# Projections of two chunks with keys, queries and values by turns

## The chip, the cores and the metric

The kernel runs on one core of a Trainium2 chip. The metric is the device time of one execution in microseconds (us); the median of the runs counts.

## The reference

The kernel computes one transformer block in float32 for 2048 tokens of width 640: attention with 32 heads of width 20, then a gated feed-forward part of width 1728. In the reference, cut to what matters here:

```python
x = A_x                                   # 1 x 2048 x 640
qkv = layernorm(x) @ wqkv                 # 640 x 1920: queries, keys, values
scores = einsum("bhqd,bhkd->bhqk", q, k) * 20 ** -0.5
o = softmax(scores) @ v
h = x + o @ wo
out = h + (silu(layernorm(h) @ w_gate) * (layernorm(h) @ w_up)) @ w_down
```

## The kernel before

**Three stages.** First the projections, up to 337 us of the profile's span: layernorm, transposes, and the product with `wqkv`. Then attention, unit by unit (a unit is a group of four heads and a chunk of 512 queries; there are 8 groups and 4 chunks). Then the output projection and the feed-forward part. The change is in the first stage alone.

**Chunks and slots.** The 2048 tokens are worked in four chunks of 512, numbered 0 to 3. The loop over a chunk (from L503) goes through a list `work` of 18 entries; an entry is called a slot here, and `slot[0] = 18 * c + j` counts them over all chunks. An entry is either a block or a value. A *block* (`query_key`, L414) computes 128 rows of keys or queries for the chunk: fifteen matmuls of 128x512 into one bank `ps_one`, as each factor is split into a high and a low part and three of the products are kept. Even blocks are keys, odd ones are queries; there are five of each. A *value* (`value`, L451) computes 128 tokens by 320 columns of values: fifteen matmuls of 128x320. There are eight of them in a chunk. Before, chunks 1 and 2 go through all keys (slots 0 to 4), all queries (5 to 9) and all values (10 to 17). Chunk 0 has queries and keys in pairs, and chunk 3 has keys, values, queries; neither is changed.

**What follows a block.** `keep` (L432) takes the next of three tiles `e` by turns (`next_e`; two own tiles and a part of `v_stk`). ACT copies the bank into it (L265), rounds it to the high part (L80), and POOL subtracts for the low part (L81). The rows go to the DRAM tensor `qk_d` in two or three DMAs on ACT's queue; `store` (L408) holds them back until the next slot's copies are issued. Values go to `v_d` in the same way through two tiles `ev` (L465), one store for two values.

**Norm and flips of the next chunk.** While chunk c is projected, DVE does the layernorm of chunk c + 1 in 15 small steps (`lns`): four of statistics, seven of the inverse root, four that apply it, one step a slot from slot 1 and two a slot from slot 5. Then, in slots 11 to 15 (`flip_at`), `flip` (L387) transposes a fifth of the normed chunk by four PE transposes into a bank `ps_one`; ACT copies it to a tile `e` (the same three by turns, L265), rounds it (L80) and POOL subtracts. There are two banks `ps_one` for blocks, values and flips together.

**Maxima by the way.** Softmax needs the maximum of the scores for each query. A part of them is worked here, to give DVE something to do: `max_pair` (L166) computes two heads' scores of 128 queries by 512 keys with two matmuls into a tile `ps_wide` (three of them by turns), and DVE reduces the tile (L175). This is called a pair. `visit(n)` (L342) tries n pairs: each slot has `visit(3)` at its end, and each block of chunks 1 to 3 has one more between its matmuls. The pairs come in a fixed order from two lists, `urgent` (the unit of group 0 and chunk 0) and `early`. For groups 1 to 7 keys and queries are read back from `qk_d` into four tiles `raw`, by `load_items` on SP's queue in four DMAs each (`stack`, L143). `stored_at` (L274) gives the slot from which a tile may be read back; a tile is loaded when the tile four places earlier in the list has had its last pair, and counts as ready two slots later. A visit whose first pair isn't ready does nothing. A pair of `early` thus waits in the program for its slot, and on the chip for its tile.

**Loads for attention.** `load_keys(0, ...)` at slot 3 and `load_queries(c)` at slot 8 read group 0's keys and queries of this chunk back from `qk_d`, on SP's queue as well.

The order of each engine's instructions is the program's order; there is no scheduler. The kernel's functions with the profile's line numbers:

Of the kernel before, what the change touches and what calls it, by code (L numbers as in the profile page):

```python
# [23 lines left out]
ND = D // P  # L24
NT = S // P
CH = 512
NC = S // CH
# [16 lines left out]
def tile_block(ctx: ExitStack, tc: tile.TileContext, x, wqkv, wo, wg, wu, wd, out):  # L44
# [102 lines left out]
    def load_keys(g, cs=slice(0, S)):  # L147

        k = keys[g] = k_stk[g % 2]
        stack(k[:, :, cs], 1, g, cs)  # L150

    def load_queries(u):

        g, c = divmod(u, NC)
        q = queries[u] = stk.tile([P, 2, CH], F32R, name="q_stk", tag="q_stk", bufs=4)
        stack(q, 0, g, slice(c * CH, (c + 1) * CH))

    def load_values(g, t0=0, t1=NT):
        values[g] = v_stk[g % 2]
        nc.sync.dma_start(  # L160
            values[g][:, t0:t1], v_d[:, g].rearrange("(t p) w -> p t w", p=P)[:, t0:t1]
        )
# [40 lines left out]
    def max_finish(u):  # L203

        m = ps_one()[: 2 * G * TPC, :P]
        nc.tensor.transpose(m, ends.pop(u).bitcast(F32).rearrange("p i n -> p (i n)"), ident)
        m2 = stk.tile([2 * G * TPC, P], F32R, name="m2", tag="m2", bufs=1)
        nc.scalar.activation(m2, m, AF.Copy)
        for b in range(2):
            for i in range(2):  # L210
                row = b * ROW + NPART + i
                first = (2 * i + b) * 2 * TPC
                nc.sync.dma_start(
                    queries[u][row : row + 1].bitcast(F32).rearrange(
                        "r j (t p) -> r (j t) p", t=TPC
                    ),
                    m2[first : first + 2 * TPC, :].bitcast(F32),
                )
# [33 lines left out]
    with tc.tile_pool(name="pa", bufs=2) as pa:  # L252
# [5 lines left out]
        def load_x(c):  # L258
            for t in range(c * TPC, (c + 1) * TPC):
                xs[t] = pa.tile([P, D], F32, name="xt", tag="xt", bufs=4)  # L260
                nc.sync.dma_start(xs[t], x[t * P : (t + 1) * P, :])
# [12 lines left out]
        def stored_at(which, g, c):  # L274

            block = ((g + 1) * GD - 1) // P
            if c == 0:
                return 2 * block + 4
            return 18 * c + 3 + block + (0 if which else ND)

        def raw_tile():
# [7 lines left out]
        def load_items():  # L289
            for n, (which, g, c, loaded, _) in enumerate(items):  # L290
                if loaded is not None:
                    continue
                if slot[0] < stored_at(which, g, c) or (n >= 4 and users[n - 4]):
                    return
                t = raw_tile().rearrange("p a b -> p (a b)")[:, : 2 * CH].rearrange(
                    "p (h n) -> p h n", h=2
                )
                stack(t, which, g, slice(c * CH, (c + 1) * CH))
                items[n][3:] = t, slot[0]
# [42 lines left out]
        def visit(n):  # L342
            load_items()
            for _ in range(n):
                for queue in (urgent, early):
                    if queue and queue[0][0]():
                        queue.pop(0)[1]()
                        break
# [3 lines left out]
        def load_w(i):  # L352

            m, n = 2 * i, min(2, 3 * ND - 2 * i)
            raw = raw_tile().bitcast(F32)
            for j in range(n):
                raws[m + j] = raw[:, :, j * P : (j + 1) * P]
            nc.sync.dma_start(
                raw[:, :, : n * P], wqkv[:, m * P : (m + n) * P].rearrange("(k p) n -> p k n", p=P)
            )  # L360

        def split_w(m):
            cs = slice(m * P, (m + 1) * P)
            engine = nc.gpsimd if m % 2 == 1 else nc.vector
            split(raws.pop(m), w_hi[:, :, cs], w_lo[:, :, cs], engine)

        def norm(c):

            mv = pa.tile([P, TPC, 2], F32, name="mv")
            r, steps = rstd_steps(pa, mv[:, :, 1], TPC, "a")  # L370

            def apply(t):
                nc.vector.tensor_scalar(
                    xs[c * TPC + t], xs[c * TPC + t], mv[:, t, 0:1], r[:, t : t + 1],
                    op0=ALU.subtract, op1=ALU.mult,
                )

            zs[c] = (
                pa.tile([P, ND, CH], F32R, name="z_hi"), pa.tile([P, ND, CH], F32R, name="z_lo")
            )  # L380
            return (
                [lambda t=t: stats(pa, xs[c * TPC + t], mv[:, t, :]) for t in range(TPC)]
                + [lambda f=f, g=g: (f(), g()) for f, g in zip(steps[::2], steps[1::2])]
                + [lambda t=t: apply(t) for t in range(TPC)]
            )

        def flip(c, k):  # L387
            ps = ps_one()
            for t in range(TPC):
                nc.tensor.transpose(  # L390
                    ps[:, t * P : (t + 1) * P], xs[c * TPC + t][:, k * P : (k + 1) * P], ident
                )
            z_hi, z_lo = (z[:, k, :] for z in zs[c])
            split_sbuf(ps, z_hi, z_lo, next_e()[:, 0].bitcast(F32))
# [102 lines left out]
        parts = [("value", *divmod(i, 2)) for i in range(2 * TPC)]  # L497
        first = [("block", 0, 1), ("none",)] + [("block", m) for m in range(2, 2 * ND)]
        some_keys = [("block", 2 * i) for i in range(ND)]
        some_queries = [("block", 2 * i + 1) for i in range(ND)]  # L500
        flip_at = (12, 11, 11)
        finish_at = 18 * NC
        for c in range(NC):  # L503
            lns = []
            work = (some_keys + some_queries if c else first) + parts
            if c == NC - 1:
                work = some_keys + parts + some_queries

                es[:] = [e for e in es if e is not third]
                es.insert(1, pa.tile([P, ND, CH], F32R, name="z_hi")[:, :2])  # L510
            for j, (kind, *which) in enumerate(work):
                slot[0] = 18 * c + j
                if c == 0 and j < 9:
                    for i in range(split_at[j], split_at[j + 1]):
                        split_w(i + 2)
                        if i % 2 == 1 and loaded < 8:
                            load_w(loaded)
                            loaded += 1
                if j == 0 and c + 1 < NC:
                    if c > 0:  # L520
                        load_x(c + 1)
                    lns = norm(c + 1)
                if which:
                    (query_key if kind == "block" else value)(c, *which)
                visit(3)
                if c == 0 and j == 6:
                    for ev in evs:
                        nc.gpsimd.memset(ev, 1.0)
                if j == (4 if c == 0 else 3):
                    load_keys(0, slice(c * CH, (c + 1) * CH))  # L530
                if j == (4 if c == 0 else 8) and c < 3:
                    load_queries(c)
                if 0 in ends:
                    finish_at = min(finish_at, slot[0] + 2)
                    if slot[0] == finish_at:
                        max_finish(0)
                if j == 14 and c == 3:
                    load_values(0)
                for _ in range(2 if j >= 5 else 1):
                    if j >= 1 and lns:  # L540
                        lns.pop(0)()
                if c + 1 < NC and 0 <= j - flip_at[c] < ND:
                    flip(c + 1, j - flip_at[c])
                if c == NC - 1 and j == 11:
                    nc.scalar.activation(
                        pa.tile([P, 1], F32, name="exp_table"), eps_t, AF.Exp
                    )
# [420 lines left out]
    for u in range(NU):  # L968
        g, c = divmod(u, NC)
        if g == NG - 1 and c >= 2:  # L970
            _, first, ln, flips, _ = ahead
# [626 lines left out]
```

## Time and profile before

| what | us |
|---|---|
| median of three runs (2109.99 to 2112.93) | 2111.07 |
| the profiled execution: its time | 2112.34 |
| its span, first to last instruction | 2110.6 |
| chunk 1, first block matmul to that of chunk 2 (89.81 to 174.96) | 85.15 |
| chunk 2 (174.96 to 263.54) | 88.58 |
| chunk 3 and up to attention (263.54 to 337.42) | 73.88 |

A profile's busy time counts an instruction from its start to its end; matmuls overlap, so PE shows as busy even where each takes longer than it need. A wait in brackets is the idle time of that engine before the instruction, with what ended it. The granted clock is the share of TensorE's full clock.

### The profile page before, as it was taken

How to read it: one execution, taken by the hardware profiler on the slowest of the kernel's cores; microseconds unless marked ns; L12 is line 12 of the kernel's file. 1: busy time of each engine (PE TensorE's matmuls, PEld its weight loads, DVE VectorE, ACT ScalarE, POOL GpSimd, SP SyncE). 2: the span in 40 equal slices, each digit the busy share in tenths (PEclk: the TensorE clock that was granted, in tenths of full speed). 3: DMA queues.
4: the chain of work that ended last, by engine and by line, in shares of the span. 5: the costliest groups of instructions: out<-in, count | busy, mean ns of one | idle time of the engine just before them, and what ended most of it. 6: DMA issues, size and time to landing. Idle time of an engine off the chain costs nothing.

```text
span 2110.6 us, 35576 instructions
## 1 busy us (share of the span) xinstructions
PE 2077.2 (98%) x12606; PEld 1205.3 (57%) x12606; DVE 1752.9 (83%) x2901; ACT 1295.9 (61%) x2571; POOL 704.8 (33%) x1009
## 2 busy tenths in 40 slices
PE   7999999999999999999999999999999999999998
PEld 5766675333333333333333333335578888888887
DVE  6999997999999999999999999996358766666676
ACT  3222216999999999999999999996743222212221
POOL 3222212343343433353420001001135434653555
PEclk9999999999999999999999999999999999999999
DMA  7565432343433524533432113132137755884542
GB/s 253 168 190 166 153 119 82 122 122 106 150 115 102 169 89 136 165 136 126 136 110 75 33 38 88 33 100 76 35 121 262 266 171 186 300 299 158 197 152 92
DMA packets 199673, 295.27 MB, mean 140 GB/s; under 512 B 46840, under 2 KB 81656, under 8 KB 198472
## 3 DMA queue, kind: packets, MB, share of 16 engines
q1 hardware_dynamic: 185912, 266.77, 39.1%
q10 hardware_dynamic: 13584, 26.23, 4.0%
q8 instruction: 101, 1.65, 0.4%
q14 instruction: 76, 0.62, 0.1%
HBM read 196.44 MB, written 95.68 MB: 138 GB/s over the span
## 4 chain that ended last, share of the span: by engine, by line
PE 89%; DVE 5%; DMA 3%; POOL 1%; issue 1%; ACT 1%; SPq 0%; ACTq 0%; POOLq 0%; DVEq 0%
PE acc L900 24%; PE ps_max L181 15%; PE ps_one L890 15%; PE ps_a L1063 15%; PE ps_b L1157 8%; PE ps_one L422 4%; DVE mx L175 3%; PE ps_one L459 2%; PE ps_wide L171 2%; PE ps_max L628 2%; PE ps_b L628 1%; DMA qk_d<-e 1%; DMA raw<-qk_d 1%; DVE mx L187 1%; DMA halves<-j_d 1%
## 5 line engine op out<-in xcount | busy, mean ns | idle before, releaser
L896 ACT ACTIVATE probs<-ps_one 128x512 f32<-128x512 f32 x2048 | 1045.4, 623 | 131.9 <-PE ps_one L890 126.9
L187 DVE TENSOR_REDUCE mx<-ps_max 128x1 f32<-128x512 f32 x1632 | 1021.0, 683 | 95.7 <-PE ps_max L181 51.9
L890 PE MATMUL ps_one<-q_stk,k_stk 62*128 62x512 f32 x2048 | 551.1, 421 | 0.7 <-ACT e L265 0.7
L900 PE MATMUL acc<-probs,v_stk 128*32 128x512 f32 x4096 | 545.2, 604 | 0.3
L181 PE MATMUL ps_max<-k_stk,q_stk 60*128 60x512 f32 x1632 | 540.5, 459 | 2.4 <-DVE mx L187 1.5
L181 PEld LDWEIGHTS ps_max<-k_stk,q_stk 60*128 60x128 f32 x1632 | 230.2, 184 | 427.6 <-DVE mx L187 411.2
L890 PEld LDWEIGHTS ps_one<-q_stk,k_stk 62*128 62x128 f32 x2048 | 299.7, 185 | 81.6 <-ACT probs L896 52.3
L175 DVE TENSOR_REDUCE mx<-ps_wide 128x2 f32<-128x1024 f32 x208 | 240.5, 1217 | 16.2 <-PE ps_wide L171 16.0
L1278 DVE TENSOR_TENSOR tmp<-ps_a,tmp 128x512 f32<-128x512 f32 x208 | 141.2, 689 | 120.2 <-PE ps_a L1063 94.5
L1157 PE MATMUL ps_b<-halves,yp 128*128 128x320 f32 x1032 | 179.3, 308 | 1.8 <-POOL yp L81 1.2
L1157 PEld LDWEIGHTS ps_b<-halves,yp 128*128 128x128 f32 x1032 | 165.1, 188 | 18.4 <-POOL yp L81 1.5
L900 PEld LDWEIGHTS acc<-probs,v_stk 128*32 128x32 f32 x4096 | 80.6, 108 | 160.2 <-issue 152.1
L198 POOL CAST both<-neg 128x16 fp32r<-128x16 f32 x32 | 6.6, 206 | 467.6 <-DVE neg L194 212.5
L1063 PE MATMUL ps_a<-t,units 128*128 128x512 f32 x624 | 162.5, 396 | 0.0
L1063 PE MATMUL ps_a<-z,units 128*128 128x512 f32 x516 | 133.8, 394 | 0.0
L1063 PEld LDWEIGHTS ps_a<-t,units 128*128 128x128 f32 x624 | 112.6, 188 | 18.6
L81 POOL TENSOR_TENSOR yp<-y,yp 128x256 fp32r<-128x256 f32 x96 | 60.3, 628 | 187.8 <-ACT yp L80 187.8
L1162 DVE TENSOR_TENSOR h<-ps_b,h 128x320 f32<-128x320 f32 x248 | 110.1, 481 | 6.8 <-PE ps_b L1157 5.4
L1063 PEld LDWEIGHTS ps_a<-z,units 128*128 128x128 f32 x516 | 93.1, 187 | 15.9
L1063 PE MATMUL ps_a<-z,lasts 128*128 128x512 f32 x324 | 92.5, 393 | 0.0
L80 ACT ACTIVATE yp<-tmp 128x512 fp32r<-128x512 f32 x40 | 25.3, 632 | 103.2 <-POOL tmp L1150 103.2
L265 ACT ACTIVATE e<-ps_one 128x512 f32<-128x512 f32 x31 | 18.5, 598 | 107.3 <-PE ps_one L422 72.4
(164 smaller groups left out, 2066.6 us busy)
## 6 DMA issues: line engine op xcount, KB each, us to landing
units<-w_d SPq DMA_DIRECT2D x186, 256.0 KB
w_d<-stage SPq DMA_DIRECT2D x106, 256.0 KB
halves<-j_d SPq DMA_DIRECT2D x70, 320.0 KB
j_d<-stage SPq DMA_DIRECT2D x42, 320.0 KB
raw<-qk_d SPq DMA_DIRECT2D x70, 160.0 KB
k_stk<-qk_d SPq DMA_DIRECT2D x64, 160.0 KB
q_stk<-qk_d SPq DMA_DIRECT2D x64, 160.0 KB
rb<-r_d SPq DMA_DIRECT2D x32, 256.0 KB
```

The costliest lines, as they stand in the source:

```text
L175: nc.vector.tensor_reduce(mx[:, :, pair, t, kc], ps, axis=AX.X, op=ALU.max)
L181: nc.tensor.matmul(ps, queries[u][rows, pair, t * P : (t + 1) * P], keys[u // NC][rows, pair, kc * CH : (kc + 1) * CH], start=True, stop=True,
L187: nc.vector.tensor_reduce(mxs[u][:, b, pair, t, kc : kc + 1], ps, axis=AX.X, op=ALU.max)
L422: nc.tensor.matmul(ps, w[:, k, m * P : (m + 1) * P], a[:, k, :], start=(n == 0 and k == 0), stop=(n == 2 and k == ND - 1),)
L628: nc.tensor.matmul(ps[:, :HALF], a[:, k, :], w[:, k, hs], start=(n == 0), stop=(n == 3 * ND - 1),)
L890: nc.tensor.matmul(ps, keys[u // NC][rows, p, kt * P : (kt + 1) * P], queries[u][rows, p, :], start=True, stop=True,)
L896: nc.scalar.activation(probs[p][:, b, :], ps, AF.Exp, scale=scale)
L900: nc.tensor.matmul(acc[32 * j : 32 * j + 32, :], values[u // NC][:, kt, j * VW : j * VW + 32], probs[j // 2][:, j % 2, :], start=(kt == 0) ...
L1063: nc.tensor.matmul(ps.rearrange("p (t n) -> p t n", t=TPC), w[k][:, i], z[k][:, :, j], start=(first and m == 0), stop=(last and m == len(n ...
L1157: nc.tensor.matmul(ps, a, b, start=(n == 0), stop=(n == len(pairs) - 1))
L1162: nc.vector.tensor_tensor(out=h, in0=ps, in1=h, op=ALU.add)
L1278: add = lambda out, ps, x: nc.vector.tensor_tensor(out=out, in0=ps, in1=x, op=ALU.add)
```

## The change

The list of chunks 1 and 2 becomes key block, query block, value, five times over, and then the last three values; the slots in which a tile counts as stored are moved along, and `load_queries` is called at slot 5 instead of 8. Keys are now in slots 0, 3, 6, 9, 12, queries in 1, 4, 7, 10, 13, values in 2, 5, 8, 11, 14, 15, 16, 17. The steps of norm, the flips and the visits stay at their slot numbers.

```diff
             block = ((g + 1) * GD - 1) // P
             if c == 0:
                 return 2 * block + 4
+            if c < NC - 1:
+                return 18 * c + 3 + 3 * block + (0 if which else 1)
             return 18 * c + 3 + block + (0 if which else ND)
...
             lns = []
-            work = (some_keys + some_queries if c else first) + parts
+            work = first + parts
+            if c:
+                work = [a for block in zip(some_keys, some_queries, parts) for a in block]
+                work += parts[ND:]
             if c == NC - 1:
                 work = some_keys + parts + some_queries
...
-                if j == (4 if c == 0 else 8) and c < 3:
+                if j == (4 if c == 0 else 5) and c < 3:
                     load_queries(c)
```

## The prediction

> **What bounds the kernel now.** The page first.
>
> ```profile
> PE 2077.2 (98%) x12606; PEld 1205.3 (57%) x12606; DVE 1752.9 (83%) x2901; ACT 1295.9 (61%) x2571; POOL 704.8 (33%) x1009
> ```
>
> PE is busy nearly throughout, so a stall of PE anywhere lengthens the run one for one. The change touches only chunks 1 and 2 of the projections. Their stages are found in the time line of PE by the first block matmul of each chunk (89.81, 174.96 and 263.54 us) and the first value matmul (145.28 and 233.46); the view by stretches, cut there, has us, then busy us of PE, PEld, DVE, ACT and POOL, the granted clock, the DMA share and GB/s.
>
> ```profile
> 89.81:145.28 55.47, 53.09 (x230) 33.37 (x229) 51.75 (x67) 11.62 (x19) 11.55 (x9) 1.00 0.64 196
> 145.28:174.96 29.68, 29.08 (x191) 23.55 (x189) 28.69 (x28) 10.33 (x20) 7.77 (x6) 1.00 0.39 125
> 174.96:233.46 58.50, 55.50 (x232) 34.41 (x230) 52.22 (x68) 12.10 (x20) 11.58 (x9) 0.97 0.61 186
> 233.46:263.54 30.08, 29.45 (x190) 23.73 (x188) 29.11 (x28) 9.85 (x19) 7.74 (x6) 1.00 0.49 154
> ```
>
> Chunk 1 takes 85.15 us and chunk 2 takes 88.58. PE and DVE are both nearly full, ACT and POOL are far from it: the two run a race, slot by slot. The time line of PE gives the price of a slot (start, us, engine and line, count, idle before in brackets).
>
> ```profile
> 89.81 1.43 PE L422 MATMUL ps_one<-z_hi,w_hi 128*128 128x512 f32 x5
> ...
> 94.09 0.97 PE L171 MATMUL ps_wide<-raw 60*128 60x512 f32 x6
> 94.99 1.43 PE L422 MATMUL ps_one<-z_hi,w_hi 128*128 128x512 f32 x5
> ...
> 100.14 1.43 PE L422 MATMUL ps_one<-z_hi,w_hi 128*128 128x512 f32 x5
> ...
> 105.88 1.45 PE L422 MATMUL ps_one<-z_hi,w_hi 128*128 128x512 f32 x5
> ...
> 111.49 0.47 PE L171 MATMUL ps_wide<-raw 60*128 60x512 f32 x1 [0.56 <-DMA raw<-qk_d]
> 113.12 0.47 PE L171 MATMUL ps_wide<-raw 60*128 60x512 f32 x1 [1.17 <-DMA raw<-qk_d]
> 113.52 1.43 PE L422 MATMUL ps_one<-z_hi,w_hi 128*128 128x512 f32 x5
> ...
> 157.03 0.97 PE L459 MATMUL ps_one<-w_hi,z_hi 128*128 128x320 f32 x5
> ...
> 159.40 0.97 PE L171 MATMUL ps_wide<-k_stk,q_stk 60*128 60x512 f32 x6
> 160.30 0.66 PE L390 MATMUL ps_one<-ident,xt 128*128 128x128 f32 x4
> 160.71 0.97 PE L459 MATMUL ps_one<-w_hi,z_hi 128*128 128x320 f32 x5
> ...
> 208.35 1.42 PE L422 MATMUL ps_one<-z_hi,w_hi 128*128 128x512 f32 x5
> ...
> 213.03 0.46 PE L171 MATMUL ps_wide<-raw 60*128 60x512 f32 x1 [1.91 <-DMA raw<-qk_d]
> ...
> 213.76 2.04 PE L422 MATMUL ps_one<-z_hi,w_lo 128*128 128x512 f32 x5
> 215.73 1.65 PE L171 MATMUL ps_wide<-raw 60*128 60x512 f32 x6
> 217.31 1.50 PE L422 MATMUL ps_one<-z_hi,w_hi 128*128 128x512 f32 x5
> ```
>
> An undisturbed block slot with four max pairs takes PE 94.99 - 89.81 = 5.18 us, 5.17 below; its last three pairs take 0.90 (94.09 to 94.99). A value slot takes 2.37 + 0.90 = 3.28, a flip 0.41 more (160.30 to 160.71). A block slot after a stats step of the next chunk's norm takes 105.88 - 100.14 = 5.74: DVE sets it. Two slots are out of line: 105.88 to 113.52 is 7.64, and 208.35 to 217.31 is 8.96; both wait for a raw tile. The chain of waits tells why (start, us, what), with the table of the waits of SP's queue.
>
> ```profile
> 105.54 5.25 DMA qk_d<-e
> 110.80 2.08 DMA raw<-qk_d
> ...
> 144.37 3.40 DVE mx L175 x3
> ...
> 190.30 3.51 DMA qk_d<-e
> 193.87 3.83 DMA raw<-qk_d
> ...
> 202.53 4.19 DMA qk_d<-e
> 206.78 0.27 SPq L143
> ...
> 207.87 5.07 DMA raw<-qk_d
> ```
> ```profile
> SPq L143 <- DMA qk_d<-e: 32.0, 14, 4.3
> ```
>
> In the built program every DMA of SP and ACT takes one of eight completion semaphores by turns and first waits for the transfer eight places earlier. So a load of a raw tile on SP stands behind a store of keys on ACT which it doesn't need, and the store is issued only when the next block's matmuls have ended. It lands 3.5 to 5.25 us after its issue, the load 2.1 to 5.1 us after that.
>
> **The change, part by part.** Nothing is added or taken away: the order listing of both kernels gives the same matmuls, copies and DMAs in all. What moves: seven of the ten blocks and three values fall into slots 1 to 10 instead of nine blocks and one value, and the flips of slots 11 to 15 stand among a value, two blocks and two values instead of five values.
>
> *The race of PE and DVE.* A pair costs DVE 3.40 / 3 = 1.133 us, so a block's four 4.53 and a value's three 3.40. Chunk 1's 63 pairs are 71.4 of its 80.4 us of DVE, chunk 2's 64 are 72.5 of 81.3: norm costs 8.9, all of it in slots 1 to 10. There DVE needs, before, 9 x 4.53 + 3.40 + 8.9 = 53.1 against PE's 9 x 5.17 + 3.28 = 49.8; after, 7 x 4.53 + 3 x 3.40 + 8.9 = 50.8 against 46.0. DVE sets both. In slots 11 to 17 PE needs, before, 7 x 3.28 + 5 x 0.41 = 25.0 against DVE's 23.8; after, 2 x 5.17 + 5 x 3.28 + 5 x 0.41 = 28.8 against 26.1. PE sets both. With slot 0 (5.17) a chunk comes to 83.3 before and 84.8 after: 1.5 us dearer, as norm is now crowded beside shorter slots and PE's surplus is left for the end. Against the trace: 85.15 less the 1.9 us by which slot 3 exceeds 5.74 is 83.3. In chunk 2 the listing shows two pairs fewer in slot 6 (the fourth group's queries, loaded in slot 5, count as ready from slot 7): minus 2.3 us of DVE; they come back in chunk 3's second query block, where PE pays 0.6 (0.90 for three) and DVE is free. Sum: 1.5 + 1.5 - 2.3 + 0.6 = **+1.3**. Bounds: the three pair buffers let PE run up to three pairs (3.4 us) ahead from one stretch into the other, which could take back both 1.5s (-1.7); and with nothing saved by the missing pairs it is +3.6.
>
> *The waits for raw tiles.* Before, they cost 1.9 us in chunk 1 and 8.96 - 5.17 = 3.8 in chunk 2, its slower matmuls included: 5.7. After, in the listing, chunk 1's sixth group has two stores among its eight loads instead of five, and is wanted a slot later, behind a value; in chunk 2 the fourth group's queries are not wanted before slot 9, since the pairs of unit 0 come in between. Both waits go. Late next is chunk 2's load of the third group's queries: its last quarter stands behind the first store of queries, issued when the first value has ended, some 13.5 us into the chunk (2 x 5.17 + 2.37, 0.44 for the value's copy and 0.3 to issue); landed after 3.5 to 5.25, the load after 2.1 to 3.8 more, at 19 to 22.5, and wanted after slot 3's matmuls, at 2 x 5.17 + 3.4 + 5.17 - 0.6 = 18.3 by PE, or 20 where DVE is behind. I take 0.8 of wait (0 to 2.5): **-4.9**, bounds -5.7 to 0 if such waits only change places.
>
> *Flips beside blocks.* Keys, queries and flips draw from one ring of three e tiles, and a tile that was stored is free when its store has landed. Before, flips stand among values, and the last block's tiles are stored long ago. After, slot 12 writes the last keys into e0, and slot 13's flip wants e0 again; the store of e0 is issued after slot 13's own copy. With M the end of slot 13's matmuls, from these rows of ACT's time line:
>
> ```profile
> 99.35 0.60 ACT L265 ACTIVATE e<-ps_one 128x512 f32<-128x512 f32 x1 [3.83 <-PE ps_one L422]
> 100.04 0.63 ACT L80 ACTIVATE e<-e 128x512 fp32r<-128x512 f32 x1
> 100.12 0.84 ACTq L411 DMA_DIRECT2D qk_d<-e  x2
> ...
> 159.51 0.44 ACT L465 ACTIVATE ev<-ps_one 128x320 f32<-128x320 f32 x1 [0.94 <-PE ps_one L459]
> ```
>
> the two pieces are issued by M + 1.6 (0.77 to the first, 0.84 for both), and land at 4.2 (between 3.5 and 5.25) later, M + 5.8. Then ACT copies the flip: its ps_one is free at M + 6.4. PE has meanwhile done three pairs, the flip, a value and three pairs, M + 0.90 + 0.41 + 3.28 = 4.6, and needs that very bank (of two) for the next flip: it waits 1.8. The next value's bank waits for the value's copy behind ACT's second pass, 6.4 + 0.63 + 0.44 = 7.5 against 5.0 without a wait: 2.5 in all, in each of two chunks, in a stretch that PE sets: **+5.0**. Bounds: 0 (landing in 2.1, as the fastest load above) to 7.2 (landing in 5.25).
>
> *The clock.* Granted clock is the column after POOL:
>
> ```profile
> 40.00:44.00 4.00, 4.00 (x11) 3.18 (x12) 3.86 (x9) 1.33 (x2) 2.92 (x3) 0.57 0.82 218
> ...
> 112.00:116.00 4.00, 2.88 (x12) 1.98 (x12) 3.40 (x6) 0.00 (x0) 0.90 (x1) 1.00 0.80 235
> 212.00:216.00 4.00, 2.97 (x9) 1.83 (x11) 1.23 (x1) 0.16 (x1) 0.00 (x0) 0.76 0.39 120
> ```
> ```profile
> 39.89 2.43 PE L422 MATMUL ps_one<-z_hi,w_hi 128*128 128x512 f32 x5 [1.87 <-DVE e L81]
> ```
>
> After pauses of 1.87 and 1.91 us the clock fell (five matmuls took 2.43 and 2.04 instead of 1.43), after 1.17 it held. The missing 0.43 x 4.00 us at 40 are 1.7 us. The new pause, 1.8 and then 0.7 with four transposes between, lies at that edge: I take one fall in the two chunks, **+1.7** (0 to 3.4). The Trainium skill, "TensorE: Matmul & The Clock Gate", section "Why this matters for your kernels", holds that gaps up to about 3 us don't bring the clock down; by it this term would be 0. The trace differs: 0.76 after 1.91 us.
>
> Sum: 1.3 - 4.9 + 5.0 + 1.7 = **+3.1 us**. The profiled execution has a span of 2110.6 and took 2112.34, 1.3 above the median of 2111.07; from the median the forecast is 2114.2 us. Nothing after 337 us changes, and no cover is there to hide a difference.
>
> **Rivals.** (1) *Slower*: the clock falls in both chunks, and the load of the third group's queries holds PE for all its 2.5 us: 3.1 + 1.7 + 1.7 = +6.5, 2117.6. It decides where the pause in slot 14 passes some 1.9 us; the store rows of 3.51 to 5.25 put it at 1.1 to 2.9. (2) *The stores land early*, in the 2.1 us of the fastest load: the flip's copy is at M + 3.7, only the value's copy is late by 0.4, the clock holds: 1.3 - 4.9 + 0.8 = -2.8, 2108.3. For it: DMA share is 0.39 and 0.49 where values stand, 0.64 and 0.61 where blocks do, and two blocks with five values lie between. Against it: no store in the chain landed under 3.5. The Trainium skill, "DMA: Bandwidth & Descriptors", section "Anatomy of one DMA", gives about 2.0 us plus size over 436 GB/s for transfers issued from GpSimd; an estimate for the largest piece, 320 KB, is 2.75 us. No row here shows that for a store. (3) *Faster*: as (2), and PE's lead carries over between the stretches, 0 new waits: -1.7 - 5.7 + 0.8 = -6.6, 2104.5. (4) *The raw waits only change places*: 3.1 + 4.9 = +8, 2119.1. That the change doesn't do what it says is excluded by the listing.
>
> **How the numbers follow.** Forecast 0.45, its own range 2112 to 2116.5; rival 1 0.22, rival 2 0.18, rival 3 0.10, rival 4 0.05. About 0.2%, 4.2 us, is what a measurement of this kernel can tell from no change. Faster by more: rival 3 and a little of 2, 0.12. Slower by more: rivals 1 and 4 and a third of the forecast, 0.42. Within: 0.46. The range from 2106.5 to 2118.5 leaves out most of 3 and 4.
>
> **What would show it.** PE's pauses for raw at 113 and 213 us are gone. In slots 13 to 15 of chunks 1 and 2 ACT's copy at L265 waits for a DMA qk_d<-e for over 2 us, and PE idles before a flip. Slots 2 to 10 are paced by DVE, and DVE idles in 11 to 15. Granted clock dips where the flips wait. If PE shows no pause there, the step on flips is wrong; if new pauses for raw appear of over 2 us, the step on loads is.

## The result, and the profile after

The changed kernel takes 2117.36 us (median of 13 runs, 2114.01 to 2120.63); the kernel before, on the same chip between them, 2109.99 (13 runs, 2107.04 to 2116.78). The ratio is 1.0031, 95% interval 1.0022 to 1.0040: slower by 0.3%, about 6.5 us. The forecast was 3.1 us slower. The profiled execution took 2120.04, 2.7 above its kernel's median, with a span of 2118.2, 7.6 more than the span before.

First the view by stretches, cut as for the kernel before at the first matmul of chunks 1, 2, 3 and of attention (columns: stretch, its us, busy us of PE, PEld, DVE, ACT and POOL, granted clock, DMA share, GB/s), and one row of the kernel before for the first ten us of attention.

```profile
90.39:176.97 86.58, 82.33 (x418) 56.58 (x417) 80.76 (x95) 21.73 (x38) 19.40 (x15) 1.00 0.55 167
176.97:267.92 90.95, 83.83 (x417) 57.70 (x415) 79.02 (x93) 21.79 (x38) 19.37 (x15) 0.98 0.56 168
267.92:343.10 75.18, 74.32 (x373) 52.91 (x371) 60.70 (x54) 15.56 (x30) 12.05 (x11) 1.00 0.41 125
343.10:353.10 10.00, 9.52 (x47) 4.07 (x49) 7.85 (x13) 8.53 (x17) 8.29 (x3) 0.83 0.56 159
```
```profile
337.42:347.42 10.00, 9.52 (x59) 4.11 (x59) 8.87 (x15) 9.43 (x19) 8.29 (x3) 1.00 0.55 159
```

Chunk 1 takes 86.58 - 85.15 = 1.4 us more than before, chunk 2 90.95 - 88.58 = 2.4 more, chunk 3 75.18 - 73.88 = 1.3 more: 5.1 of the 7.6. The rest lies outside: 90.39 - 89.81 = 0.6 before chunk 1, whose order is not changed, and 1.9 after chunk 3, where the clock fell once (0.83 of full over ten us, 1.7 us lost) and did not in the profile before.

In chunk 2 PE is busy 7.1 us less than the stretch is long. Where it stood shows in PE's time line (start, us, engine and line, count, idle before in brackets): the flips of chunk 1, the tiles of chunk 2, the flips of chunk 2, and the second block of queries in chunk 3.

```profile
165.97 0.66 PE L392 MATMUL ps_one<-ident,xt 128*128 128x128 f32 x4 [1.16 <-ACT e L265]
...
195.08 0.50 PE L171 MATMUL ps_wide<-raw 60*128 60x512 f32 x2 [1.79 <-DVE mx L175]
...
198.81 0.47 PE L171 MATMUL ps_wide<-raw 60*128 60x512 f32 x1 [1.62 <-DMA raw<-qk_d]
199.93 0.93 PE L171 MATMUL ps_wide<-raw 60*128 60x512 f32 x5 [0.65 <-DMA raw<-qk_d]
200.78 2.33 PE L424 MATMUL ps_one<-z_hi,w_hi 128*128 128x512 f32 x5
...
256.35 0.66 PE L392 MATMUL ps_one<-ident,xt 128*128 128x128 f32 x4 [1.68 <-ACT e L265]
...
327.20 1.42 PE L424 MATMUL ps_one<-z_hi,w_hi 128*128 128x512 f32 x5
...
331.90 1.43 PE L424 MATMUL ps_one<-z_hi,w_hi 128*128 128x512 f32 x5
```

The pauses for raw at 113 and 213 us are gone, as said. In their place stand three pauses within 7 us in chunk 2's slots 3 and 4, 1.79 + 1.62 + 0.65 = 4.1 us, and behind them five matmuls take 2.33 instead of 1.43: the clock. Before the flips PE waits for ACT, and ACT's time line says for what:

```profile
161.00 1.70 ACTq L413 DMA_DIRECT2D qk_d<-e  x2
165.31 0.60 ACT L265 ACTIVATE e<-ps_one 128x512 f32<-128x512 f32 x1 [3.71 <-DMA qk_d<-e]
...
250.90 1.06 ACTq L413 DMA_DIRECT2D qk_d<-e  x2
255.70 0.60 ACT L265 ACTIVATE e<-ps_one 128x512 f32<-128x512 f32 x1 [4.25 <-DMA qk_d<-e]
```

That is the step on flips as told: the copy of slot 13's flip stands 3.7 and 4.3 us behind the store of the keys whose tile it wants, which is back 4.3 and 4.8 us after its issue began. The prediction took 4.2 from the end of the issue on, so the tile came free somewhat earlier than it had it.

The pauses in slots 3 and 4 have a chain of their own. The chain of waits of the changed kernel, and the waits of SP's queue between 176 and 204 us (us in total, times, longest):

```profile
189.88 0.31 ACTq L413
...
190.23 6.57 DMA qk_d<-e
...
196.82 3.09 DMA raw<-qk_d
...
199.93 0.93 PE ps_wide L171 x5
```
```profile
SPq L261 <- DMA v_d<-ev: 7.0, 1, 7.0
```

One of the four loads of x (L261) stands 7.0 us behind the store of the last values of chunk 1. SP's queue is in order, so the loads of raw tiles behind it are late too. DVE meanwhile needs the rows (its time line):

```profile
192.81 0.89 DVE L116 BATCH_NORM_STATS2 st<-xt 128x6 f32<-128x320 f32 x2 [2.36 <-DMA xt<-in_A_x]
```

That is the 1.79 us of PE behind DVE. And then many transfers run at once (the same view by stretches of four us; the last three figures are clock, DMA share and GB/s):

```profile
186.00:190.00 4.00, 4.00 (x26) 3.04 (x26) 3.47 (x4) 1.42 (x3) 1.30 (x1) 1.00 0.46 89
190.00:194.00 4.00, 3.23 (x15) 1.80 (x12) 1.60 (x5) 0.25 (x1) 0.00 (x0) 1.00 1.00 317
```

The DMA engines move 89 GB/s up to 190 us and are full from there to 194. The store of q0, issued at 189.9, falls into just this stretch and takes 6.57 us; the third group's queries load behind it.

### The profile page after: what moved, and what is told of

The parts are those of the page before. It is cut to its first block, busy times and chain, and to the rows that moved or that the text cites. A ratio compares the mean times of both kernels' runs of the same rounds, so it can differ in the third digit from the quotient of the medians.

```text
span 2118.2 us, 35577 instructions
## 1 busy us (share of the span) xinstructions
PE 2079.0 (98%) x12606; PEld 1205.0 (57%) x12606; DVE 1752.2 (83%) x2901; ACT 1295.4 (61%) x2571; POOL 705.0 (33%) x1009
## 4 chain that ended last, share of the span: by engine, by line
PE 87%; DVE 7%; DMA 4%; issue 1%; SPq 1%; ACT 1%; POOL 0%; ACTq 0%; POOLq 0%; DVEq 0%
PE acc L905 24%; PE ps_max L181 15%; PE ps_one L895 15%; PE ps_a L1068 14%; PE ps_b L1162 7%; PE ps_one L424 4%; DVE mx L175 4%; PE ps_max L633 2%; PE ps_wide L171 2%; PE ps_one L461 2%; DMA halves<-j_d 1%; PE ps_b L633 1%; DMA qk_d<-e 1%; DVE mx L187 1%; DMA units<-w_d 0%
```

## The experiments

The theory before the experiments: three things make up the 5.1 us, namely the flips' wait for the tile of the stored keys, a new wait for raw tiles that comes of SP's loads standing behind ACT's stores, and the race of PE and DVE as the order sets it. The rivals: that waits only change places when one is removed, that the transfers themselves collide, or that blocks and values by turns cost PE or ACT something by themselves. Brackets behind a ratio hold its 95% interval. The chunk times of each kernel come from one profile.

**Flips with a tile of their own.** The changed kernel, where the flips of chunks 1 and 2 copy into a free end of `v_stk`:

```diff
+    flipped = v_stk[0].rearrange("p t w -> p (t w)")[:, 2 * CH :]
...
-            split_sbuf(ps, z_hi, z_lo, next_e()[:, 0].bitcast(F32))
+            split_sbuf(ps, z_hi, z_lo, flipped if c > 1 else next_e()[:, 0].bitcast(F32))
```

> The changed kernel, but the flips for chunks 2 and 3 copy into a tile of their own (the free end of v_stk) and no longer draw from the ring of three e tiles. Theory: PE's two pauses before a flip (1.23 + 0.57 us in chunk 1, 1.74 + 0.58 in chunk 2, by the profile after) come from the store of e0 that hasn't landed. They go: chunk 1 takes 84.8 us instead of 86.6, chunk 2 88.6 instead of 91.0, and the run is 4 us faster than the changed kernel, +3.3 against before (ratio 1.0016). Rival: that stretch has slack, since DVE has pairs to catch up, and the wait only moves: both chunks stay within 0.5 us and the run stays at +7 (1.0033).

Measured: ratio 0.9999 (0.9989 to 1.0010), less than the 1.0016 expected. Chunks 1 and 2 in the view by stretches:

```profile
88.23:172.97 84.74, 81.97 (x418) 56.56 (x417) 80.79 (x95) 21.90 (x38) 19.39 (x15) 1.00 0.55 170
172.97:262.32 89.35, 84.10 (x416) 58.02 (x415) 78.93 (x93) 21.95 (x38) 19.38 (x15) 0.96 0.58 171
```

Chunk 1 falls from 86.58 to 84.74: the flips' wait was 1.8 there, and nothing came in its place. In chunk 2 slot 14 falls from 6.01 to 3.68, 2.3 us, while slots 3 and 4 grow from 9.86 + 6.76 to 10.77 + 6.53. The wait for raw is another one, and chunk 2 misses its 88.6. The three chunks together are still 1.6 us longer than in the kernel before; the profiled run made that up outside them, beginning chunk 1 at 88.23 instead of 89.81 us (the end of the next section says more on this).

**Rows of x two slots earlier.** The changed kernel; `load_x` for the chunk after the next moves from slot 0 to slot 16 of the chunk before:

```diff
-                    if c > 0:
-                        load_x(c + 1)
...
+                if j == 16 and c + 2 < NC:
+                    load_x(c + 2)
```

> The changed kernel, but x for the chunk after next is loaded at slot 16 of the chunk before instead of slot 0. Theory: in chunk 2 DVE waits 2.36 us for x in front of slot 3's pairs, and this, with the raw wait behind it (1.62 + 0.65) and the fall of the clock (slot 4: 2.33 and 1.79 us for 1.43 and 1.07), makes slots 3 and 4 cost 4.2 us over chunk 1's; with x there, the queue of loads is free when the third group's queries are due: slots 3 and 4 back to 6.5 + 5.5 us, chunk 2 at 87, the run at +3.5 against before (1.0017). Rival: the raw tile is late by its own (it stands behind the store of q0, which took 6.57 us), and x only shares the wait: slot 3 stays above 9 us and the run at +6 to +7 (1.003).

Measured: ratio 1.0013 (1.0004 to 1.0022). Chunk 2 in the view by stretches:

```profile
177.06:264.35 87.29, 82.79 (x418) 56.73 (x416) 78.76 (x93) 22.08 (x39) 19.36 (x15) 1.00 0.61 176
```

Chunk 2 falls from 90.95 to 87.29, with the clock at 1.00. The store of q0, its second piece issued at 191.47 us here, has landed by 195.68, when the load that waited for it is issued: 4.2 us instead of 6.57, at a DMA share of 0.67 to 0.78 instead of 1.00. The late rows of x are thus a link of the chain. The load itself is the same; only its place in the queue has changed.

**Both together.** The changed kernel with the last two edits:

> The changed kernel with both pauses taken away: the flips of chunks 1 and 2 copy into their own tile, and the rows of x for chunks 2 and 3 are loaded two slots before the chunk begins. Theory (the change costs its two pauses, and beside them the order itself is no dearer than the waits of the kernel before): chunk 1 as with the flip tile alone, 84.7 us; chunk 2 as with the early rows alone less its flip pause, 87.3 - 2.3 = 85.0; chunk 3 75.2. That is 244.9 against 247.6 in the kernel before: ratio 0.9987. Rival (the two pauses stand in one chain and only one of the gains is to be had, or the order loses elsewhere): as either edit alone, 0.9999 to 1.0013.

Measured: ratio 0.9996 (0.9982 to 1.0011), medians 2110.65 and 2111.07. Chunks 1 and 2 by stretches:

```profile
88.90:173.67 84.77, 82.25 (x418) 56.73 (x417) 80.79 (x95) 21.82 (x38) 19.41 (x15) 1.00 0.54 162
173.67:258.73 85.06, 82.41 (x416) 56.83 (x414) 78.68 (x93) 21.94 (x38) 19.39 (x15) 1.00 0.62 179
```

Both chunks are as expected to 0.1 us, so the gains add. The ratio tells less: its interval holds the theory's 0.9987 as well as the rival's value.

**Keys and queries by turns, values last.** The half of the change that leaves blocks together:

```diff
-                return 18 * c + 3 + 3 * block + (0 if which else 1)
+                return 18 * c + 3 + 2 * block + (0 if which else 1)
...
-                work = [a for block in zip(some_keys, some_queries, parts) for a in block]
-                work += parts[ND:]
+                work = [a for block in zip(some_keys, some_queries) for a in block] + parts
```

> Half of the change: in chunks 1 and 2 keys and queries by turns (slots 0 to 9), the eight values after them as before. Theory: the race of PE and DVE is that of before (1.5 us a chunk back), flips stand among values again (4.1 us back), so only waits for raw tiles and xt can differ: chunk 1 at 83 to 85 us, chunk 2 at 85 to 89, the run between -3 and +2 us of before (0.9985 to 1.001). Rival: what costs is that queries are stored as early as keys and the loads stand behind more stores; then the loss stays, +5 or more (1.0024 or more).

Measured: ratio 1.0013 (1.0000 to 1.0025), between the two; the profiled run is the slowest of its twelve. In it the values' slots are as before, no flip waits, and chunk 3 is back at 73.85. But chunk 1 takes 88.8 us and chunk 2 89.8, both above what the theory allowed. Slots 3 and 4 of chunk 1 take 9.39 + 7.09 us where the kernel before has 7.64 + 5.19. Two rows of PE's time line, the pause and the block after it:

```profile
112.18 0.76 PE L171 MATMUL ps_wide<-raw 60*128 60x512 f32 x1 [2.32 <-DMA raw<-qk_d]
...
114.19 2.50 PE L424 MATMUL ps_one<-z_hi,w_hi 128*128 128x512 f32 x5
```

So this version has no flip that waits and pays new waits for raw tiles. As a test of the race it is inconclusive.

**The blocks' stores on GpSimd's queue, old order.** If loads wait because they share completion semaphores with ACT's stores, they must stop when SP's loads no longer stand eight places behind those. In `keep` of the kernel before:

```diff
-            store(*pieces, queue=nc.sync if (c, m) == (NC - 1, 2 * ND - 1) else nc.scalar)
+            store(*pieces, queue=nc.sync if (c, m) == (NC - 1, 2 * ND - 1) else (
+                nc.gpsimd if 0 < c < NC - 1 else nc.scalar))
```

> The kernel before, but the stores of keys and queries of chunks 1 and 2 are issued on POOL's queue instead of ACT's. Theory: loads of raw tiles on SP wait for a store only because both queues take the same eight completion semaphores by turns; with the stores off them, slot 3 of chunk 1 goes from 7.64 to 5.8 us and slot 6 of chunk 2 from 8.96 to 5.4: 83.3 and 84.8 us for the chunks, the run 5 us faster than before (0.9976). Rival: the loads are late because the DMA engines are full (share 0.6 to 0.9 there); then both slots stay, and POOL's issue may add to it: 0 to +3 us (1.000 to 1.0015).

Measured: ratio 0.9974 (0.9964 to 0.9984), chunk 1 83.39, chunk 2 84.26, chunk 3 73.85, and PE waits for no raw tile. The old order without its waits is at the 83.3 us that the prediction worked out for chunk 1.

One rival to that reading is that stores from GpSimd's queue merely land sooner. The trace's records of the DMAs name the semaphore that each completes on: in the kernel before, the DMAs of SP and ACT between 89 and 260 us take the same eight between them; with every store on GpSimd's queue (the kernels further below, old order and new) the stores take eight others, and they land no sooner. For the new order the view of DMAs has, as count, KB each and median us from issue to landing:

```profile
qk_d<-e POOLq DMA_DIRECT2D x12, 320.0 KB, 5.3
```

In the old order that median is 4.6. So the loads no longer wait, though the stores take as long as those that were waited for before.

**The same in the new order.** The changed kernel with the flips' own tile and the edit of `keep` above:

> The changed kernel with the flips' own tile, and with the stores of chunks 1 and 2 on GpSimd's queue, so that loads share no semaphore with a store just issued. It stands beside the kernel before with the same stores (chunks 83.4, 84.3 and 73.85, ratio 0.9974): what is left between the two is the order itself, without any wait for a store. Theory: chunk 1 84.7 (the race, +1.35), chunk 2 84.3 (race and two pairs dropped), chunk 3 75.2 (the pairs come back, +1.3): together +2.6 us, ratio 0.9987. Rival (the new pause in chunk 2 comes of the transfers themselves, not of the shared semaphores): chunk 2 stays at 87 to 88.6, ratio 1.0002 or more.

Measured: ratio 0.9992 (0.9979 to 1.0005); chunk 1 84.70, chunk 3 75.16 as expected, but chunk 2 86.72, near the rival's 87. The chain of waits shows a pause of the same kind, and ACT's time line whose store stands at its head:

```profile
188.27 4.62 DMA qk_d<-v_stk
...
192.90 0.27 SPq L143
...
193.22 3.12 DMA raw<-qk_d
```
```profile
188.27 1.29 ACTq L414 DMA_DIRECT2D qk_d<-v_stk  x2
```

The store was issued on ACT's queue, not on GpSimd's: a block's store is sent off by the next slot's call, and behind a block of queries that slot is a value, whose own `store` still named ACT. In the old order that happens once a chunk, in the new one five times (the expectation below speaks of two, the traces show five). The edit had missed the store that counts, so the next two kernels move those as well.

**Every store on GpSimd's queue, both orders.** In `value`, for chunks 1 and 2, on top of the edit of `keep`; once in the changed kernel with the flips' own tile, once in the kernel before:

```diff
-                store((v_d[rows], ev))
+                store((v_d[rows], ev), queue=nc.gpsimd if 0 < c < NC - 1 else nc.scalar)
             else:
-                store()
+                store(queue=nc.gpsimd if 0 < c < NC - 1 else nc.scalar)
```

> The changed kernel with the flips' own tile, and now every store of chunks 1 and 2 on GpSimd's queue, those too that a value's call sends off (with the blocks' alone there, two stores of chunk 2 still left on ScalarE's queue, and the load that PE waited for stood behind one of them). The rows of x are loaded at the chunk's start as in the changed kernel. Theory (the new pause in chunk 2 comes of semaphores shared with a store just issued): chunk 1 84.7, chunk 2 84.3, chunk 3 75.2, 1.3 us less over chunks 1 to 3 than in chunks 1 to 3 of the kernel before at 247.6 less its waits, so ratio about 0.9985. Rival (the pause comes of the transfers of x, stores and loads that fall together): chunk 2 at 86.5 or more, ratio 0.9995 or more.

> The kernel before with every store of chunks 1 and 2 on GpSimd's queue, those of a value's call too. Theory: as with the blocks' stores alone there, chunks 83.4, 84.3 and 73.9, ratio 0.9974, and 2.6 us below the changed order with the same stores. Rival (values' stores behind GpSimd's other work come late, or the order makes no difference once no load stands behind a store): within 0.5 us of the changed order.

Measured: new order 2109.23 us, ratio 0.9979 (0.9967 to 0.9991); old order 2105.73, ratio 0.9963 (0.9950 to 0.9975). The new order by stretches, chunks 1 to 3, then chunk 1 cut where slot 1 and slot 11 begin:

```profile
88.71:173.40 84.69, 81.97 (x417) 56.55 (x417) 80.81 (x95) 21.94 (x38) 35.04 (x43) 1.00 0.55 169
173.40:257.67 84.27, 82.06 (x417) 56.74 (x415) 78.79 (x93) 21.94 (x38) 34.93 (x43) 1.00 0.60 182
257.67:332.80 75.13, 74.29 (x373) 52.89 (x371) 60.71 (x54) 15.54 (x30) 12.03 (x11) 1.00 0.41 126
...
93.89:144.77 50.88, 48.16 (x227) 31.36 (x225) 49.72 (x67) 10.31 (x18) 18.11 (x23) 1.00 0.59 185
144.77:173.40 28.63, 28.63 (x171) 21.86 (x170) 26.57 (x25) 10.94 (x20) 16.93 (x20) 1.00 0.47 144
```

The old order with the same stores:

```profile
88.72:172.06 83.34, 82.22 (x417) 57.04 (x416) 80.20 (x94) 21.94 (x38) 34.91 (x43) 1.00 0.56 173
172.06:256.24 84.18, 82.89 (x421) 57.06 (x419) 81.19 (x95) 21.94 (x38) 34.77 (x43) 1.00 0.61 185
256.24:329.80 73.56, 72.69 (x370) 52.66 (x369) 58.39 (x52) 15.55 (x30) 12.00 (x11) 1.00 0.42 124
...
93.90:145.66 51.76, 51.29 (x228) 32.82 (x226) 50.27 (x67) 12.03 (x20) 25.28 (x33) 1.00 0.67 203
145.66:172.06 26.40, 25.74 (x169) 20.88 (x167) 25.42 (x24) 9.21 (x17) 9.63 (x11) 1.00 0.35 120
```

Chunk 2 of the new order is at the expected 84.3, with the rows of x loaded where the changed kernel loads them. So the rival, by which the pause comes of the transfers themselves, is out: they are the same here. What SP waits for there, from 173.4 to 204 us, has no store in it:

```profile
SPq L143 <- PE ps_wide L171: 16.0, 4, 5.2
SPq L143 <- DMA raw<-qk_d: 2.9, 5, 1.1
SPq L262 <- DMA raw<-qk_d: 0.5, 1, 0.5
```

Neither order now waits for a store, and the new one is 1.35 + 0.09 + 1.57 = 3.0 us longer over the three chunks: the price of the order itself. The medians differ by 3.5, the two profiled spans by 6.0, as the clock fell at the start of attention in the new order's profile (0.66 over ten us) and not in the other (1.00). The old order with its stores on GpSimd's queue beats both kernels of the case.

**Without the race.** Both orders again, with the blocks' stores on GpSimd's queue (and the flips' own tile in the new order), and each pair reduced over half of its columns:

```diff
-        nc.vector.tensor_reduce(mx[:, :, pair, t, kc], ps, axis=AX.X, op=ALU.max)
+        nc.vector.tensor_reduce(mx[:, :, pair, t, kc], ps[:, :, : CH // 2], axis=AX.X, op=ALU.max)
```

> The kernel with the flips' own tile and the stores on GpSimd's queue, in the changed order, with each reduction of a pair over half of its columns (the maxima over the other half are left out), so that DVE is nowhere full in chunks 1 and 2. Beside it runs the kernel before with the same stores and the same half reductions. Theory (the order costs 1.35 us in chunk 1 only because it crowds DVE's norm and leaves PE's surplus for the end): with DVE out of it both orders take what PE needs, 10 x 5.17 + 8 x 3.28 + 5 x 0.41 = 80.0 us in chunk 1, and differ by under 0.3. Rival (blocks and values by turns cost PE or ACT something by themselves): chunk 1 is longer by about 1.35 in the changed order here too.

> The kernel before with the stores of chunks 1 and 2 on GpSimd's queue and each reduction of a pair over half of its columns (the maxima over the other half are left out). Theory: chunk 1 at PE's own need, 80.0 us, as in the changed order with the same edits; chunk 2 80.0 and two pairs more than in the changed order (0.6). Rival: chunk 1 1.35 us shorter than in the changed order.

Measured: ratios 0.9936 (0.9914 to 0.9959) and 0.9909 (0.9878 to 0.9940). Chunks 1 and 2 in the new order, the one long pause of PE there, and the two chunks in the old order:

```profile
86.90:167.02 80.12, 80.12 (x419) 56.73 (x417) 49.60 (x95) 21.95 (x38) 27.79 (x30) 1.00 0.58 180
167.02:249.18 82.16, 80.11 (x417) 56.68 (x415) 49.04 (x92) 21.96 (x38) 27.55 (x30) 1.00 0.62 186
```
```profile
187.53 0.93 PE L171 MATMUL ps_wide<-raw 60*128 60x512 f32 x5 [2.05 <-DMA raw<-qk_d]
```
```profile
85.27:165.38 80.11, 80.11 (x418) 56.60 (x416) 50.44 (x94) 21.94 (x38) 32.28 (x38) 1.00 0.58 181
165.38:245.18 79.80, 79.80 (x421) 56.76 (x419) 51.10 (x95) 21.95 (x38) 32.08 (x38) 1.00 0.63 194
```

In chunk 1 DVE is busy 50 of 80 us, PE all of it, and the two orders take the same, at the 80.0 worked out. The 1.35 us of chunk 1 exist only where DVE is nearly full: that is the race, and the rival by which turns cost PE something by themselves is out. Chunk 2 is 2.4 us longer in the new order, where 80.0 or less was expected. Slot 3 takes 188.39 - 180.66 = 7.73 us there instead of 5.17, with the pause shown, behind a block's store that this kernel too still issues on ACT's queue; the other slots together are within 0.2 us of PE's own need. The medians differ by 5.3 us, of which this is about half.

**The new order in chunk 1 alone.**

```diff
-            if c < NC - 1:
+            if c == 1:
                 return 18 * c + 3 + 3 * block + (0 if which else 1)
...
-            work = first + parts
-            if c:
+            work = (some_keys + some_queries if c else first) + parts
+            if c == 1:
...
-                if j == (4 if c == 0 else 5) and c < 3:
+                if j == (4, 5, 8, 8)[c] and c < 3:
```

> The changed order in chunk 1 alone, nothing else edited; chunk 2 as in the kernel before. Theory: chunk 1 as in the changed kernel, 86.6 (its flip pause 1.8 and the race 1.35, less the wait of 1.9 that goes), chunk 2 as before, 88.6 (its wait of 3.8 stays), chunk 3 73.9 as no pairs are dropped: +1.4 us, ratio 1.0007. Rival (what the change does in one chunk depends on the other): chunk 2 differs from 88.6 by over 1 us, or chunk 3 is at 75.2.

Measured: ratio 1.0004 (0.9992 to 1.0017). Chunks 1 and 2 by stretches:

```profile
90.95:177.17 86.22, 82.28 (x418) 56.58 (x417) 80.69 (x95) 21.73 (x38) 19.37 (x15) 1.00 0.55 167
177.17:264.67 87.50, 84.87 (x421) 58.19 (x419) 80.87 (x95) 21.96 (x38) 19.30 (x15) 0.98 0.59 179
```

Chunk 1 and chunk 3 (73.55) do what the theory says. Chunk 2 waits in the same slot as before (8.34 us, before 8.96), but is 1.1 us shorter in all, just past the rival's bound: 0.6 of it is in that slot and 0.6 in slot 3 (5.52 against 6.09). So a chunk that waits for loads can differ by about a microsecond between two profiles of the same code, and the figures of the next table are good to no more than that.

## Why the prediction was right or wrong

The direction was right and 2117.36 us lies inside the wide range, but above the forecast's own range of 2112 to 2116.5. The number is nearest to rival 1 (2117.6), and that is luck: of what rival 1 adds, the raw tiles did hold PE for over 2 us, but the clock did not fall at the flips, and 2.5 us came from outside the changed chunks.

| term | predicted | measured |
|---|---|---|
| race of PE and DVE, moved pairs | +1.3 | 1.35 + 0.1 + 1.3 = +2.75 |
| waits for raw tiles | -4.9 | -6.2 + 4.4 = -1.8 |
| flips beside blocks | +5.0 | 1.9 + 2.3 = +4.2 |
| clock, at the flips | +1.7 | 0 |
| chunks 1 to 3 | +3.1 | +5.1 |
| outside them | 0 | +2.5 |

The measured column goes by the pair with every store on GpSimd's queue, which has no waits: chunks 1 and 2 of each kernel less those of its order there. Before: 85.15 - 83.34 = 1.8 and 88.58 - 84.18 = 4.4, 6.2 in all; the race is the difference of the two orders there, and for chunk 3 that of the two kernels of the case. After: 86.58 - 84.69 = 1.9, all of it the flips', and 90.95 - 84.27 = 6.7, of which slot 14's 2.3 are the flips' and 4.4 the raw tiles'.

- **The waits for raw tiles are the step that failed**, in its size: "I take 0.8 of wait (0 to 2.5)". Place and mechanism were as told, the last quarter of the third group's queries behind the first store of q0, but chunk 2 paid 4.4. By the prediction's own sign (new pauses for raw of over 2 us) the step is wrong: they are 1.62 + 0.65 = 2.27 us. The step gave that store 3.5 to 5.25 us to land and put the loads of x at nothing: the store's 6.57 us fell into the rows of x, themselves late by a store of values. DVE's wait for those rows, 1.79 us of PE, was not in the sum at all, and the pauses took the clock down: slot 4 takes 6.76 us where it takes 5.52 without waits. Where the rows of x come early and the flips have their own tile, chunk 2 takes 85.06 against 84.27 without any store's wait: 0.8, just what the step had taken. So what it left out is the rows of x, which stand in the same queue of SP and wait for stores in the same way. What carried the step, that loads wait for stores through shared semaphores, is shown: with the stores on another queue both orders are free of it, though the stores land no sooner there.
- **The race** is right where it was worked out best: slots 1 to 10 of chunk 1 take 50.88 us against a predicted 50.8 and slots 11 to 17 28.63 against 28.8; chunk 1 came to 83.34 and 84.69 against 83.3 and 84.8. The old order's two stretches, 51.76 and 26.40, were put at 53.1 and 25.0: right in sum, but not in their parts. DVE is busy 50.27 us in the first and 25.42 in the second (put at 53.1 and 23.8), so some of its reductions ran over into the second stretch, as the pair buffers allow; there neither engine is full (PE 25.74 of 26.40). In the new order DVE is busy 49.72 us of the first stretch and PE all 28.63 of the second, as told. The two pairs that move were costed wrongly at both ends. Chunk 2's slot 6 without them takes 4.71 us where chunk 1's takes 6.20, 1.5 less and not 2.3, as PE sets that slot once they are gone; in the whole chunk they save 1.35 - 0.1 = 1.25. In chunk 3's second query block they cost 331.90 - 327.20 = 4.70 against 3.52 before, 1.2 and not 0.6, as a pair between a block's matmuls, or alone at its end, is dearer than one of three in a row.
- **The flips** are right in place and cause, and nearly in size: 4.2 us of 5.0.
- **The clock** held at the flips, after pauses of 1.16 and 1.68 us, where one fall had been taken. The fall in chunk 2 is that of the raw tiles' pause and stood in chunk 2 before as well, so it makes no difference. The Trainium skill, "TensorE: Matmul & The Clock Gate", section "Why this matters for your kernels", sets the bound for one gap at about 3 us. At the flips the trace agrees; after 1.79, 1.62 and 0.65 us within 7 us of time it does not, nor after the 2.32 us of the kernel with values last, behind which five matmuls took 2.50 us; after the 2.05 us in chunk 2 of the half reductions the clock held. Once PE has begun, no profile here has one lone gap of over 3 us.
- **Outside the chunks** nothing was forecast, and 2.5 us came. 0.6 of them had come before the first changed slot. At the start of attention the clock fell in five of the seven profiles of kernels with the new order in both chunks, and in two of the six others. The pause there is 0.69 us in all thirteen. These counts are too small to be told from chance, so a third of the difference of the spans stays open.

A second place shows the same. At 40 us, in chunk 0, whose order no kernel here changes, PE waits for DVE. The clock fell there in seven of the thirteen profiles, after pauses of 1.87 to 2.29 us, and held in the six others, after 1.39, 1.41, 1.77 and also 2.22, 2.27 and 2.38. This is the row of one where it held, to be set beside the prediction's row at 39.89 where it fell:

```profile
40.35 1.45 PE L422 MATMUL ps_one<-z_hi,w_hi 128*128 128x512 f32 x5 [2.22 <-DVE e L81]
```

With full reductions, chunk 1 begins at 88.2 to 88.9 us where the clock held and at 89.8 to 91.0 where it fell: 0.9 to 2.7 us that no edit makes. The granted clock is on record for single runs too. Within one kernel a run is some 2.0 us longer for each 0.001 of clock less; the mean is 0.99723 for the changed kernel's 13 runs and 0.99786 for 81 runs of the kernel before beside the experiments. By these numbers an estimate of 1.2 us of the difference is clock.

## What to carry to other kernels

A load that must wait for a store it doesn't read should first be looked for in the completion semaphores and the order of the issuing queue, not in the data; taking the stores to a third queue cost nothing that shows in the chunks here and gave 0.37% (interval 0.25 to 0.50%). A moved store is to be priced with all transfers in flight where it lands, and with every load, of whatever tensor, that stands behind it in a queue. Two engines that are both nearly full are costed stretch by stretch: the longer one counts in each, and an order that leaves one engine's surplus for the end pays for it there.

## What the runs showed of the hardware

A store of keys or queries on ACT's queue (two or three pieces) was waited for 3.4 to 5.3 us in most places and 6.57 where it met the rows of x (DMA share 1.00); on GpSimd's queue its pieces of 320 KB took 4.6 and 5.3 us in the median. TensorE's clock fell after pauses that add up to 4.1 us in 7, and after single ones of 1.87 to 2.34; it held after 1.68, and in other profiles after 2.05 to 2.38. A start of attention with the same 0.69 us of pause had a granted clock of 1.00 in one profile and 0.83 in the other. What decides it is not settled by these runs.
